# Two queues for the first reads, and another order of the first block's preparation, in a two-layer transformer kernel

## The chip, the cores and the metric

The kernel runs on one core of a Trainium2 chip. The metric is the device time of one launch in microseconds (us). The engines are TensorE (PE, with its weight loads PEld), VectorE (DVE), ScalarE (ACT), GpSimd (POOL) and SyncE (SP, which computes nothing and issues DMAs).

## The reference

Two layers, each an attention block and a gated block on 2048 tokens of 448 features, with the same weights in both layers:

```python
x = A_x                                     # [1, 2048, 448] f32
for _ in range(2):
    x = x + attention(layernorm(x))         # 16 heads of 28, qkv = x @ wqkv (448 x 1344), @ wo
    h = layernorm(x)
    x = x + (sigmoid(h @ w_gate) * (h @ w_up)) @ w_down      # inner size 1792
```

The layer norm has no scale and no offset. Everything is f32 in and out.

## The kernel before

**Number format.** Matrix products run on f16 operands. Each f32 operand is split into a high f16 part and a low f16 part (the f32 value less the high part), and a product is three matmuls: high by high, high by low, low by high. Weights are scaled by a power of two before the split; the power comes from the mean square of the matrix, so all of a weight block has to be read and squared before its first split. The features are four rows of 128: rows 0 to 2 are whole, row 3 holds 64 features, and its free half carries low parts (the "tail").

**Blocks.** The tokens are four blocks of four tiles of 128 tokens. For the projections a block has to stand with its features on the partitions, so its normalised tokens are turned.

**The order.** The kernel's order is written out by hand: each engine executes its instructions in program order, and DMAs issued by one engine enter one queue in that order. A read that reuses one of the completion semaphores waits in its issuing engine until the earlier transfer on that semaphore has landed. Buffers come from rings of slots (`big`, `qrt`).

**The head**, which the change touches, ends at the first projection matmuls:

- `load_x(t, n)` reads n token tiles from tile t on SyncE's queue. Tiles 0 to 3 (the first block) are read singly.
- `wq.read(j)` reads a third of wqkv (0 query, 1 key, 2 value) through `load_rows`; the query third in four pieces: two rows, one row, and the tail's 64 features twice.
- `first.stats(j)` takes mean and variance of a tile on DVE (`BATCH_NORM_STATS2`, `BATCH_NORM_AGGREGATE`) and the inverse root on POOL; `first.scale(t)` writes the normalised tile on DVE; `first.turn(t)` turns it on PE, four transposes into four PSUM banks, each bank holding one feature row of all four tiles.
- `first.turned_high(kts)` copies such banks as high parts (`xhl`); `first.turned_low(kts)` subtracts for the low parts, on DVE.
- `wq.measure_first(i)` squares and sums the query weights in three pieces (two on ScalarE, the last on DVE); `wq.sum_first(i)` adds them over the partitions on PE; `powers` makes the scale `up`.
- `wq.high_cols` scales weight columns to their high part on ScalarE, `wq.low_cols` makes the low part on DVE. `wq.measure(1)`, further on, squares the key weights on ScalarE.
- `keep_busy(n)` runs n matmuls of zeros (`still`) on PE, whose result nobody reads.

The first projection tile is eleven matmuls (`qkp`, line 564). Their order is that in which parts become ready: rows 0 to 2 of high by high, low parts of rows 0 and 1, the low weights, the low part of row 2, the tails.

Of the kernel before, what the change touches and what calls it, by code (L numbers as in the profile page):

```python
# [15 lines left out]
AF = mybir.ActivationFunctionType  # L16
# [3 lines left out]
P = 128  # L20
S = 2048
D = 448
# [5 lines left out]
TB = NT // NB  # L28
# [90 lines left out]
def interleaved_layers(ctx: ExitStack, tc: tile.TileContext, x_in, wqkv, wo, w_gate, w_up,  # L119
                       w_down, out):  # L120
    nc = tc.nc
# [6 lines left out]
    big = Slots(spool, "s", N_SLOTS)  # L128
# [22 lines left out]
    def bank(i, name):  # L151
        return psum(f"bank{i}", name, [P, 512])


    x = cpool.tile([P, NT, D], F32, name="x")
# [5 lines left out]
    warm = cpool.tile([P, 1], F32, name="warm")  # L161
# [10 lines left out]
    x_src = x_in[0].rearrange("(p t) d -> p t d", t=NT)  # L172
    x_dst = out[0].rearrange("(p t) d -> p t d", t=NT)

    def load_x(t, n):
        nc.sync.dma_start(x[:, t:t + n, :], x_src[:, t:t + n, :])

    nc.vector.memset(still, 0.0)
    nc.vector.memset(warm, 0.0)
    nc.scalar.activation(warm, warm, AF.Square)  # L180
    make_identity(nc, ident)
    nc.gpsimd.memset(nhalf, -0.5)
    nc.gpsimd.memset(ones, 1.0)
# [3 lines left out]
    def tables():  # L187


        nc.gpsimd.memset(ind_f, 1.0)  # L190
        for j in range(2):
            v = ind_f[:, 4 * j:4 * j + 4, :]
            off = -64 * j
            nc.gpsimd.affine_select(out=v, in_=v, compare_op=ALU.is_ge, fill=0.0, base=off,
                                    pattern=[[P, 4], [-DH, H]], channel_multiplier=1)
            nc.gpsimd.affine_select(out=v, in_=v, compare_op=ALU.is_ge, fill=0.0,
                                    base=DH - 1 - off, pattern=[[-P, 4], [DH, H]],
                                    channel_multiplier=-1)
        nc.gpsimd.memset(ind[:, 8:, :], 0.0)
        nc.gpsimd.tensor_copy(ind[:, 0:8, :], ind_f)  # L200
        qrt.put(ind_f)
        units = big.get("units", [2, S], F16)
        nc.gpsimd.memset(units, UNIT)
        nc.gpsimd.dma_start(unit_scr, units)
        big.put(units)


    def load_rows(dst, src, c0, n, queue=nc.sync, parted=False):

        for a, b in ((0, 2), (2, 3)) if parted else ((0, 3),):  # L210
            queue.dma_start(dst[:, a:b, :],
                            src[a * P:b * P, c0:c0 + n].rearrange("(s p) n -> p s n", p=P))
        queue.dma_start(dst[0:64, 3, :], src[384:448, c0:c0 + n])
        queue.dma_start(dst[64:128, 3, :], src[384:448, c0:c0 + n])

    def split(hi, lo, raw):

# [24 lines left out]
    def powers(c, n, squares):  # L242


        c = slice(c, c + n)
        nc.vector.tensor_scalar(pw[:, c], squares.bitcast(I32), 24, 23,
                                op0=ALU.logical_shift_right, op1=ALU.logical_shift_left)
        nc.vector.tensor_scalar(up.bitcast(I32)[:, c], pw[:, c], -1.0, float(203 << 23),
                                op0=ALU.mult, op1=ALU.add)
# [7 lines left out]
    def keep_busy(n=1):  # L257
        pm = bank(2, "still")
        for i in range(n):
            c = slice(P * (i % 4), P * (i % 4) + P)  # L260
            nc.tensor.matmul(pm, still[:, c], still, start=(i == 0), stop=(i == n - 1))

    class Block:
# [256 lines left out]
                nc.scalar.copy(self.raw[0:n, kt, :], pt[0:n])  # L520
            big.put(self.xn)

        def turned_high(self, kts=range(4), engine=None):
            for kt in kts:
                if kt not in self.pt:
                    continue
                to, pt = ((self.hi[:, kt, :], self.pt[kt]) if kt < 3 else
                          (self.tail[0:64], self.pt[kt][0:64]))
                if engine is nc.vector:
                    nc.vector.tensor_copy(to, pt)  # L530
                else:
                    nc.scalar.copy(to, pt)

        def turned_low(self, kts=range(4)):
            for kt in kts:
                if kt not in self.pt:
                    continue
                pt = self.pt[kt]
                if kt < 3:
                    nc.vector.tensor_tensor(self.lo[:, kt, :], pt, self.hi[:, kt, :],  # L540
                                            op=ALU.subtract)
                else:
                    nc.vector.tensor_tensor(self.tail[64:128], pt[0:64], self.tail[0:64],
                                            op=ALU.subtract)

        def drop(self):
# [53 lines left out]
    class WeightsQKV:  # L600
# [3 lines left out]

            self.raw = []

        def read(self, j):
            self.raw.append(big.get("wraw", [P, 4, D]))
            load_rows(self.raw[j], wqkv, j * D, D, parted=(j == 0))

        def measure_first(self, i):

# [10 lines left out]
        def sum_first(self, i):  # L623
            if i == 0:
                self.first = bank(3, "sums")[:, 0:1]
            nc.tensor.matmul(self.first, ones, first_sums[:, i:i + 1], start=(i == 0),
                             stop=(i == 2))
            if i == 2:
                powers(0, 1, self.first)

        def measure(self, j):
            junk = big.get("junk", [P, 4, D], BF16)
# [292 lines left out]
    class Measure:  # L925
# [9 lines left out]
        def read(self, n=1):  # L935
            for _ in range(n):
                kind, j = self.to_read.popleft()
                t = big.get("raw", [P, 2048])
                n = {"o": 4, "d": min(4, NF - 4 * j), "gu": 0}[kind]
                v = t[:, 0:n * D].rearrange("p (s n) -> p s n", n=D)  # L940
                queue = nc.sync if kind == "o" or j < 3 and kind == "d" else nc.gpsimd
                if kind == "gu":
                    v = t.rearrange("p (w s c) -> p w s c", w=2, s=4)
                    for i, w in enumerate((w_gate, w_up)):
                        load_rows(v[:, i], w, 0, 2 * P, queue)
                elif kind == "o":
                    load_rows(v, wo, 0, D, queue)
                else:
                    queue.dma_start(v, w_down[j * 512:j * 512 + n * P, :].rearrange(
                        "(s p) n -> p s n", p=P))  # L950
                self.rows.append((kind, t, n * D))
# [868 lines left out]
    expect_jump(0)  # L1820
    wq = WeightsQKV()
    wq.tiles()
    first = Block(0)
    begun = [first]
    for t in range(TB):
        load_x(t, 1)
    wq.read(0)
    wq.read(1)
    load_x(TB, TB)
    wq.read(2)  # L1830
    load_x(2 * TB, 2 * TB)
    keep_busy(11)
    wq.measure_first(0)
    first.begin()
    first.turn_banks(4, range(4))
    first.parts()
    first.stats(0)
    first.stats(1)
    for t in range(TB):
        first.scale(t)  # L1840
        first.turn(t)
        keep_busy(2)
        if t == 0:
            first.stats(2)
            first.stats(3)
    wq.sum_first(0)
    first.turned_high([0], nc.vector)
    wq.measure_first(1)
    wq.measure_first(2)
    wq.sum_first(1)  # L1850
    first.turned_high([1, 2])
    first.turned_low([0])
    keep_busy(2)
    wq.sum_first(2)
    tables()
    keep_busy(3)
    wq.high_cols(0, 0, P, slice(0, 1))
    wq.high_cols(0, 0, P, slice(1, 4))
    first.turned_high([3])
    wq.high_cols(0, P, D)  # L1860
    first.turned_low([1])
    wq.low_cols(0, 0, P)
# [3 lines left out]
    for layer in range(LAYERS):  # L1866
# [4 lines left out]
        wq = WeightsQKV()  # L1871
# [34 lines left out]
```

## Time and profile before

| | |
|---|---|
| median of three runs | 1894.76 us (1894.62 to 1895.75) |
| span of the profiled execution (its own time is not given) | 1893.0 us |
| PE busy | 1886.5 us of the span |
| DVE, ACT, POOL busy | 1430.7, 1382.7, 231.5 us |
| HBM read, written | 207.88 MB, 50.85 MB |
| granted TensorE clock | 1.000 |

The page gives busy time for the whole span. The head is read from the timeline, which lists instructions in order: start, duration, engine, line, operation, output and input, count, and in brackets how long the engine had been idle and what released it. Lines "SPq" are DMA issues, not transfers. The view by stretches gives each engine's busy time in a stretch, the granted clock, the share of the 16 DMA engines' time, and GB/s.

### The profile page before, as it was taken

What the parts mean: (1) busy time and instruction counts of PE and PEld (TensorE: products, weight loads), DVE (VectorE), ACT (ScalarE), POOL (GpSimd) and SP (SyncE); (2) the same over time, 40 slices, a digit from 0 to 9 for tenths busy, and PEclk for the clock granted to TensorE, in tenths of its full rate; (3) what the DMA queues carried; (4) which work ended last, traced back from release to release, by engine and by line L of the source; (5) the groups of instructions that cost most, each with busy time, mean ns of one, the idle gap of its engine ahead of it and who ended that gap; (6) DMA issues with size and microseconds to landing.
All of it is one profiled execution on the core that took longest, in us unless ns stands there. A gap on an engine that the chain in (4) does not pass through costs nothing. (4 is left out here: it accounts for less than half of the span.)

```text
span 1893.0 us, 56282 instructions
## 1 busy us (share of the span) xinstructions
PE 1886.5 (100%) x24254; PEld 1323.1 (70%) x24254; DVE 1430.7 (76%) x2835; ACT 1382.7 (73%) x1772; POOL 231.5 (12%) x453
## 2 busy tenths in 40 slices
PE   9999999999999999999999999999999999999999
PEld 4455555555556799999954556667666567999998
DVE  7758989898976688787564487787778676887664
ACT  5569999999993566555345799999999745565541
POOL 3023112222101111111100000000000020121110
PEclk9999999999999999999999999999999999999999
DMA  7676454334323566646734322122120245666553
GB/s 247 194 212 166 132 137 128 107 119 129 103 88 121 192 205 235 231 181 238 251 96 134 90 52 47 32 52 52 31 48 24 67 160 174 218 251 223 208 208 142
DMA packets 110882, 270.86 MB, mean 143 GB/s; under 512 B 13214, under 2 KB 67838, under 8 KB 110496
## 3 DMA queue, kind: packets, MB, share of 16 engines
q0 software_dynamic: 31776, 158.51, 23.4%
q1 hardware_dynamic: 78288, 108.20, 20.3%
q8 instruction: 192, 3.15, 0.7%
q10 hardware_dynamic: 560, 0.46, 0.1%
q14 instruction: 66, 0.54, 0.1%
HBM read 207.88 MB, written 50.85 MB: 137 GB/s over the span
## 5 line engine op out<-in xcount | busy, mean ns | idle before, releaser
L1222 ACT ACTIVATE prob_s<-sc 128x1536 f32<-128x1536 f32 (+1 forms) x657 | 887.9, 1487 | 6.6 <-PE sc L1207 5.9
L1258 PE MATMUL acc<-prob_s,val_s 128*32 128x256 f32 (+3 forms) x7700 | 569.9, 383 | 0.0
L1207 PE MATMUL sc<-qp_s 114*32 114x512 f16 x7868 | 553.2, 379 | 0.0
L579 PEld LDWEIGHTS <-gu_s 128*128 128x128 f16 x4368 | 426.9, 98 | 46.8 <-issue 0.4
L1207 PEld LDWEIGHTS <-qp_s 114*32 114x32 f16 x8192 | 272.7, 95 | 203.4 <-issue 88.3
L1258 PEld LDWEIGHTS acc<-prob_s,val_s 128*32 128x32 f32 x7700 | 272.3, 110 | 142.9 <-issue 13.6
L579 PE MATMUL chain<-xwide_s,gu_s 128*128 128x256 f16 x2016 | 247.5, 273 | 0.0
L1552 PE MATMUL dnp<-dn_s,hparts_s 128*128 128x224 f16 x2016 | 225.2, 259 | 0.0
L1552 PEld LDWEIGHTS <-hparts_s 128*128 128x128 f16 x2016 | 194.0, 98 | 4.4
L1238 DVE SCALAR_TENSOR_TENSOR power_q<-power_q,expo_q 128x512 f32<-128x512 f32 x243 | 168.2, 692 | 8.3
L1625 ACT COPY one_q<-chain 128x256 f32<-128x256 f32 x224 | 82.4, 371 | 121.4 <-PE chain L579 120.8
L1641 DVE TENSOR_TENSOR one_q<-side,one_q 128x512 f32<-128x512 f32 x112 | 72.2, 686 | 101.8 <-PE side L579 101.5
L579 PE MATMUL side<-xshort_s,gu_s 128*128 128x256 f16 x1120 | 140.5, 273 | 0.0
L564 PE MATMUL qkp<-xhl_s,wqk_s 128*128 128x512 f16 x616 | 138.1, 379 | 0.7 <-ACT wqk_s L231 0.2
L564 PEld LDWEIGHTS <-wqk_s 128*128 128x128 f16 x616 | 60.1, 98 | 69.8 <-ACT wqk_s L231 1.1
L1437 POOL DMA_DIRECT2D gu_s<-gu_parts x104 | 56.0, 538 | 430.5 <-PE side L579 424.5
L1287 DVE STREAM_TRANSPOSE oturned_q<-acc 128x512 f32<-128x512 f32 x32 | 22.9, 716 | 97.1 <-PE acc L1258 96.9
L1258 PE MATMUL acc<-power_q,val_s 128*32 128x256 f32 (+3 forms) x300 | 94.2, 396 | 0.0
L579 PE MATMUL side<-xwide_s,gu_s 128*128 128x256 f16 x672 | 91.6, 273 | 0.0
L1505 ACT CAST hparts_s<-hsums_q 128x256 f16<-128x256 f32 (+1 forms) x136 | 65.0, 494 | 30.2 <-DVE hsums_q L1517 20.2
L756 ACT ACTIVATE qkhl_q<-qkp 128x512 f16<-128x512 f32 x56 | 33.2, 593 | 71.9 <-PE qkp L564 68.3
L1652 ACT ACTIVATE one_q<-one_q 128x512 f32<-128x512 f32 x56 | 35.2, 629 | 64.3 <-DVE one_q L1641 64.3
(218 smaller groups left out, 2318.0 us busy)
## 6 DMA issues: line engine op xcount, KB each, us to landing
gu_s<-gu_parts POOLq DMA_DIRECT2D x104, 800.0 KB, 6.0
dn_s<-dn_parts POOLq DMA_DIRECT2D x42, 784.0 KB, 7.8
qp_s<-qk_scr SPq DMA_DIRECT2D x96, 224.0 KB
qk_scr<-qkhl_q SPq DMA_DIRECT2D x56, 256.0 KB
gu_parts<-pack_s POOLq DMA_DIRECT2D x14, 800.0 KB, 3.8
xt_scr<-xs_s SPq DMA_DIRECT2D x48, 224.0 KB
xraw_s<-xt_scr SPq DMA_DIRECT2D x12, 768.0 KB
qp_s<-qk_scr SPq DMA_DIRECT2D x64, 112.0 KB
```

Source lines behind the costliest of these rows:

```text
L564: nc.tensor.matmul(pm, w, x, start=(i == 0), stop=(i == len(terms) - 1))
L579: nc.tensor.matmul(pm, a, x, start=(first and i == 0), stop=(i == len(terms) - 1), skip_group_check=True)
L1207: nc.tensor.matmul(ps[32 * j:32 * j + 32, :], hd.k[:, keys], hd.q[:, qb * W:(qb + 1) * W], start=True, stop=True, tile_position=(0, 32 * j))
L1222: nc.scalar.activation(prob[:, 0:n, :], ps[:, 0:n, :], AF.Exp, scale=exp_scale)
L1238: nc.vector.scalar_tensor_tensor(p, p, c[k], y, op0=ALU.add, op1=ALU.mult)
L1258: nc.tensor.matmul(acc[qb * VC:(qb + 1) * VC, s], v[:, kc % TB, h, :], probs[c * NB + qb][:, s], start=(kc == 0 and a == 0), stop=(kc == N ...
L1437: queue.dma_start(self.gu[-1][m], gu_parts[p, m])
L1505: nc.scalar.copy(to[:, :, 0], a)
L1552: nc.tensor.matmul(pm, a[:, x, t], w[:, p, y], start=(begin and n == 0 and (j == 0 or alone)), stop=(n == 2), skip_group_check=True)
L1625: nc.scalar.copy(to, pm)
L1641: nc.vector.tensor_tensor(one[m], side[m], one[m], op=ALU.add)
L1652: nc.scalar.activation(out, v, AF.Sigmoid, scale=gate_scale)
```

## The change

The four single token tiles are now read by SyncE as the first thing in the program, and the query weights by ScalarE at the same time (`wq.read(0, nc.scalar)`); ScalarE's first activation, which loads its table, stands behind those reads. The key weights, tiles 4 to 7, the value weights and tiles 8 to 15 are read by SyncE behind `read_behind`: a one-column memset on DVE, placed after tile 2's statistics, into the slot that the key weights will take.

The squares of the query weights on ScalarE, and their sums on PE, now stand ahead of every copy of turned tiles on ScalarE; DVE's square of the last piece stands ahead of its first copy. The high copies are made in two halves: tiles 0 and 1 early, tiles 2 and 3 after the scale has been made; on ScalarE the second halves stand behind the first two weight scales. The statistics of tile 3 now follow the scale of tile 1. There are 17 zero matmuls in the head instead of 24. Behind the head every engine has the same instructions in the same order.

```diff
-    def load_x(t, n):
-        nc.sync.dma_start(x[:, t:t + n, :], x_src[:, t:t + n, :])
-
+    def load_x(t, n, queue=nc.sync):
+        queue.dma_start(x[:, t:t + n, :], x_src[:, t:t + n, :])
+
+    for t in range(TB):
+        load_x(t, 1)
     nc.vector.memset(still, 0.0)
     nc.vector.memset(warm, 0.0)
-    nc.scalar.activation(warm, warm, AF.Square)
...
-        def turned_high(self, kts=range(4), engine=None):
+        def turned_high(self, kts=range(4), engine=None, js=range(TB)):
+            c = slice(js[0] * P, (js[-1] + 1) * P)
...
+        def read_behind(self):
+
+            raw = big.get("wraw", [P, 4, D])
+            nc.vector.memset(raw[:, 0, 0:1], 0.0)
+            big.put_next(raw)
...
-            if i == 2:
-                powers(0, 1, self.first)
+
+        def scale_first(self):
+            powers(0, 1, self.first)
...
     wq.tiles()
+    wq.read(0, nc.scalar)
     first = Block(0)
     begun = [first]
-    for t in range(TB):
-        load_x(t, 1)
-    wq.read(0)
-    wq.read(1)
-    load_x(TB, TB)
-    wq.read(2)
-    load_x(2 * TB, 2 * TB)
-    keep_busy(11)
-    wq.measure_first(0)
+    nc.scalar.activation(warm, warm, AF.Square)
+    keep_busy(8)
     first.begin()
     first.turn_banks(4, range(4))
     first.parts()
     first.stats(0)
     first.stats(1)
     for t in range(TB):
+        if t == TB - 1:
+            wq.measure_first(2)
+            for i in range(3):
+                wq.sum_first(i)
+            first.turned_high([0], nc.vector, (0, 1))
+            keep_busy(1)
         first.scale(t)
         first.turn(t)
-        keep_busy(2)
         if t == 0:
             first.stats(2)
+            wq.read_behind()
+            wq.read(1)
+            load_x(TB, TB)
+            wq.read(2)
+            load_x(2 * TB, 2 * TB)
+            wq.measure_first(0)
+            wq.measure_first(1)
+        if t == 1:
+            first.turned_high(range(1, 4), None, (0, 1))
             first.stats(3)
-    wq.sum_first(0)
-    first.turned_high([0], nc.vector)
-    wq.measure_first(1)
-    wq.measure_first(2)
-    wq.sum_first(1)
-    first.turned_high([1, 2])
-    first.turned_low([0])
+        if t < TB - 1:
+            keep_busy(2)
+    wq.scale_first()
+    first.turned_high([0], nc.vector, (2, 3))
     keep_busy(2)
-    wq.sum_first(2)
     tables()
-    keep_busy(3)
     wq.high_cols(0, 0, P, slice(0, 1))
     wq.high_cols(0, 0, P, slice(1, 4))
-    first.turned_high([3])
+    first.turned_high([1, 2], None, (2, 3))
+    first.turned_low([0])
+    first.turned_high([3], None, (2, 3))
     wq.high_cols(0, P, D)
     first.turned_low([1])
     wq.low_cols(0, 0, P)
```

More of the change, by code (lines that the diff above doesn't have):

```diff
@@ L212, in load_rows @@
                             src[a * P:b * P, c0:c0 + n].rearrange("(s p) n -> p s n", p=P))
-        queue.dma_start(dst[0:64, 3, :], src[384:448, c0:c0 + n])
-        queue.dma_start(dst[64:128, 3, :], src[384:448, c0:c0 + n])
+        for r in (0, 64):
+            queue.dma_start(dst[r:r + 64, 3, :], src[384:448, c0:c0 + n])
     def split(hi, lo, raw):
@@ L526, in turned_high @@
                     continue
-                to, pt = ((self.hi[:, kt, :], self.pt[kt]) if kt < 3 else
-                          (self.tail[0:64], self.pt[kt][0:64]))
+                to, pt = ((self.hi[:, kt, c], self.pt[kt][:, c]) if kt < 3 else
+                          (self.tail[0:64, c], self.pt[kt][0:64, c]))
                 if engine is nc.vector:
@@ L532, in turned_high, with turned_low @@
                     nc.scalar.copy(to, pt)
-        def turned_low(self, kts=range(4)):
+        def turned_low(self, kts=range(4), js=range(TB)):
+            c = slice(js[0] * P, (js[-1] + 1) * P)
             for kt in kts:
@@ L537, in turned_low @@
                     continue
-                pt = self.pt[kt]
+                pt = self.pt[kt][:, c]
                 if kt < 3:
-                    nc.vector.tensor_tensor(self.lo[:, kt, :], pt, self.hi[:, kt, :],
+                    nc.vector.tensor_tensor(self.lo[:, kt, c], pt, self.hi[:, kt, c],
                                             op=ALU.subtract)
                 else:
-                    nc.vector.tensor_tensor(self.tail[64:128], pt[0:64], self.tail[0:64],
+                    nc.vector.tensor_tensor(self.tail[64:128, c], pt[0:64], self.tail[0:64, c],
                                             op=ALU.subtract)
@@ L605, in tiles, with read @@
             self.raw = []
-        def read(self, j):
+        def read(self, j, queue=nc.sync):
             self.raw.append(big.get("wraw", [P, 4, D]))
-            load_rows(self.raw[j], wqkv, j * D, D, parted=(j == 0))
+            load_rows(self.raw[j], wqkv, j * D, D, queue, parted=(j == 0))
+        def read_behind(self):
+            raw = big.get("wraw", [P, 4, D])
+            nc.vector.memset(raw[:, 0, 0:1], 0.0)
+            big.put_next(raw)
         def measure_first(self, i):
```

## The prediction

> **What bounds the kernel now.** I read the page first, then the busy time by stretches of the head, then the order of time there. The page: its span of 1893.0 us lies 1.76 us below the median of the three runs, 1894.76 us; the profiled execution's own time is not given, so I add a change of the span to the median.
>
> ```profile
> span 1893.0 us, 56282 instructions
> ...
> PE 1886.5 (100%) x24254; PEld 1323.1 (70%) x24254; DVE 1430.7 (76%) x2835; ACT 1382.7 (73%) x1772; POOL 231.5 (12%) x453
> ```
>
> TensorE has no rest of the span to hide anything in. The stretches (busy time and count by engine, granted clock, DMA share, GB/s):
>
> ```profile
> 0.00:5.00 5.00, 3.75 (x9) 1.34 (x10) 1.73 (x6) 1.49 (x2) 1.43 (x11) 1.00 0.55 159
> ...
> 2.50:3.50 1.00, 1.00 (x4) 0.44 (x3) 0.02 (x1) 0.00 (x0) 0.00 (x0) 1.00 1.08 375
> 3.50:5.00 1.50, 1.50 (x5) 0.46 (x4) 1.43 (x4) 0.00 (x0) 0.49 (x2) 1.00 0.79 215
> 5.00:10.00 5.00, 4.22 (x21) 2.47 (x20) 3.43 (x9) 0.93 (x2) 3.64 (x10) 1.00 1.02 301
> 10.00:15.00 5.00, 4.68 (x27) 2.48 (x26) 4.14 (x10) 4.09 (x10) 4.50 (x12) 1.00 1.05 324
> ...
> 25.00:30.00 5.00, 5.00 (x27) 2.58 (x26) 4.51 (x15) 3.51 (x7) 1.81 (x4) 1.00 0.31 105
> ```
>
> From 25 us PE is busy throughout, so a microsecond in the head is a microsecond at the end, and nothing behind the head is touched: its instructions stand in the same order on every engine. Up to 10 us the busy resource is the DMA, which outside the dip at 3.5 to 5 us is at a share of 1. What arrives, and what is issued, in order of time:
>
> ```profile
> 0.79 1.28 ACT L180 ACT_TABLE_LOAD   x1 [0.79 <-PEq L1893]
> 0.80 1.82 SPq L176 DMA_DIRECT2D x<-in_A_x_dram  x4
> ...
> 1.25 4.87 PE L261 MATMUL still<-still_q 128*128 128x512 f16 x11 [1.25 <-DVE warm L179]
> ...
> 2.65 0.94 SPq L211 DMA_DIRECT2D wraw_s<-in_A_wqkv_dram  x2
> ...
> 4.88 0.59 SPq L211 DMA_DIRECT2D wraw_s<-in_A_wqkv_dram  x1
> ...
> 5.92 1.08 PE L508 MATMUL turn<-ident,xn_s 128*128 128x128 f32 x4
> ...
> 6.79 0.74 PE L261 MATMUL still<-still_q 128*128 128x512 f16 x2
> ...
> 7.01 0.63 DVE L495 BATCH_NORM_STATS2 st<-x 128x6 f32<-128x448 f32 x1 [0.43 <-DMA x<-in_A_x_dram]
> ...
> 8.31 0.66 PE L508 MATMUL turn<-ident,xn_s 128*128 128x128 f32 x4 [0.78 <-DVE xn_s L320]
> ...
> 8.81 0.59 PE L261 MATMUL still<-still_q 128*128 128x512 f16 x2
> ...
> 9.07 0.95 ACT L620 ACTIVATE junk_q<-wraw_s 128x896 bf16<-128x896 f32 x1 [6.78 <-DMA wraw_s<-in_A_wqkv_dram]
> ...
> 10.93 0.58 SPq L176 DMA_DIRECT2D x<-in_A_x_dram  x1
> ```
>
> The fourth token tile is there at 7.01, the first half of the query weights at 9.07, and all of them just before 10.93 (that read waits in the program for the semaphore of their last piece). In bytes: a tile is 0.229 MB, the query weights 0.917 MB; so 0.917, 1.376 and 1.835 MB in order. The chain from there:
>
> ```profile
> 7.68 0.18 DVE L496 BATCH_NORM_AGGREGATE mv<-st 128x2 f32<-128x6 f32 x1
> ...
> 8.39 0.70 POOL L500 TENSOR_TENSOR rs<-rs,nhalf 128x1 f32<-128x1 f32 x1
> ...
> 9.12 0.51 DVE L320 TENSOR_SCALAR xn_s<-x,mv,rs 128x448 f32<-128x448 f32 x1 [0.44 <-POOL rs L500]
> ...
> 10.11 0.60 PE L508 MATMUL turn<-ident,xn_s 128*128 128x128 f32 x4
> ...
> 10.42 0.69 DVE L530 CAST xhl_s<-turn 128x512 f16<-128x512 f32 x1 [0.79 <-PE turn L508]
> ...
> 10.97 0.50 PE L626 MATMUL sums<-first_sums,ones 128*128 128x1 f32 x4
> ...
> 11.03 0.61 DVE L617 CUSTOM_DVE_ANT_0 junk_q<-wraw_s 128x448 bf16<-128x448 f32 x1
> ...
> 11.56 0.69 DVE L540 TENSOR_TENSOR xhl_s<-turn,xhl_s 128x512 f16<-128x512 f32 x1
> ...
> 12.35 0.15 DVE L248 TENSOR_SCALAR up<-pw 128x1 int32<-128x1 int32 x1
> ...
> 12.54 0.91 ACT L231 ACTIVATE wqk_s<-wraw_s,up 128x128 f16<-128x128 f32 x2 [0.91 <-DVE up L248]
> ...
> 12.99 2.41 PE L564 MATMUL qkp<-xhl_s,wqk_s 128*128 128x512 f16 x9 [0.20 <-ACT wqk_s L231]
> ...
> 13.48 0.75 DVE L234 SCALAR_TENSOR_TENSOR wqk_s<-wraw_s,up,wqk_s 128x512 f16<-128x512 f32 x1 [0.38 <-ACT wqk_s L231]
> ...
> 14.86 0.68 DVE L543 TENSOR_TENSOR xhl_s<-turn,xhl_s 64x512 f16<-64x512 f32 x1
> ...
> 15.08 1.69 ACT L633 ACTIVATE junk_s<-wraw_s 128x1792 bf16<-128x1792 f32 x1
> ...
> 15.60 2.97 PE L564 MATMUL qkp<-xhl_s,wqk_s 128*128 128x512 f16 x13 [0.20 <-DVE xhl_s L543]
> ```
>
> The first projection matmul is at 12.99, but the first tile can't end before DVE's last subtraction (L543) ends at 15.54: PE goes on at 15.60. That point is what I move. The tokens' own branch has room: cast at 10.42, before the weights' square at 11.03.
>
> **The change part by part.** *Transfers.* ScalarE issues its four weight reads from about 0.8 (its table load had that place; at 0.59 us for such an issue, four take 2.4, and the table load ends near 4.5, with ScalarE idle until 9.07 anyway: nothing). So weights start some 1.8 us sooner, but on DMA engines that x already fills. With equal turns the k-th part of x lands when twice its bytes have been moved: tile 1 (half of all) when 0.917 MB had arrived before, 7.0; tile 2 when 1.376 MB had, 9.1; tile 3 with the last weights. That end was 10.9. It comes forward by the dip: 21% of 1.5 us = 0.3. That gives 10.6, with 10.9 as the late bound. The early bound is the mean rate: 159 GB/s over 5 us are 0.8 MB, the rest at 301 GB/s is through at 8.45. [...] 8.45 + 1.6 less the dip is 9.7, which I take, since its row is the landing of the same tile; 8.45 and 10.9 stay for the range.
>
> [...]
>
> *From tile 3 (landing T) to PE's point.* DVE: statistics 0.85 (7.01 to 7.86). Then it has, in its new order, the scale of tile 2 (0.51), the square of the weights' last quarter (0.61), half a cast, and the scale of tile 3. A half cast has its nearest rows here:
>
> ```profile
> L1648 DVE TENSOR_TENSOR two_q<-side,two_q 128x256 f32<-128x256 f32 x112 | 42.2, 418 | 0.0
> L1625 ACT COPY two_q<-chain 128x256 f32<-128x256 f32 x112 | 41.2, 372 | 40.3 <-PE chain L579 39.9
> ```
>
> 0.42. So T + 2.4, past POOL's T + 2.1 (0.85 and 7.86 to 9.09). Scale to T + 2.9; 0.5 to the turned tile (9.63 to 10.42 less PE's queue), half cast 0.42: T + 3.8. Then five old steps in their old order: 0.69, 0.69, 0.75, 0.68, 0.68 = 3.5. PE's point is T + 7.4; break-even T is 8.2. At T = 9.7 it is 17.1: 1.5 later.
>
> *From the last weights (landing Tw).* The square now stands ahead of half cast, scale, turn, half cast and the five steps: 0.61 + 0.42 + 0.51 + 0.5 + 0.42 + 3.5 = Tw + 6.0, where before it was 10.9 + 4.7. With the weights at the same 9.7 that is 15.7: not last. The edit "weights squared ahead of all copies" therefore gains nothing while tile 3 is late; it puts a scale and two half casts behind Tw that lay ahead of it.
>
> *PE's queue, an added wait.* Turning tile 2 now writes banks of which ScalarE still copies the first half, so it waits for three half copies (3 x 0.37 = 1.1), and these stand on ScalarE behind both weight squares. Behind that wait on PE: two still matmuls, the three sums, one still matmul, turning tile 3. From tile 2 at 9.1: statistics 0.85, scale 0.51, turn 0.6, copies about 1.0, the rest of the turn and two stills 0.6, sums 0.5, still 0.2, turning to its first bank 0.3, half cast 0.42, 3.5: 17.6. With tile 2 0.5 sooner (dip and the rest of what moves T) 17.1. So this wait ends level with the DVE chain, and the two hide each other.
>
> *PE's pace.* The still matmuls ran at 4.87/11 = 0.44 us, those at 6.79 took 0.74 a pair, those at 8.81 0.59: PE speeds up after some 5.5 us of work, while the granted clock reads 1.00 all along. Eight instead of eleven end at 1.25 + 8 x 0.44 = 4.8, still at the slow pace, and the first turn now waits behind tile 1's statistics (DVE order): 7.0 + 0.85 + 0.51 = 8.4. PE rests 3.6 us. Slow, each group of turn and stills costs 1.08 + 0.44 instead of 0.6 + 0.44 and stands in the queue above: 0.5 for one, 1.3 for two and the last one. I take 0.7.
>
> *Reads held back.* SyncE's key-weight read now waits for a one-column memset behind tile 2's statistics, about 10; behind it in SP's queue stand six more reads and then the stores. Key weights, 0.917 MB at 324 GB/s = 2.8, land near 14.5; ScalarE's square of them comes at 15.08 + 2. The later tokens and values follow on a queue that stays full: covered by some 2 us; without that cover it would count in full. ScalarE has three half copies (1.1) between its first scales and that square, where one tail copy stood: 0.5 more in front of the first tile's evacuation, of which PE takes no notice as long as the next tile has another bank: nothing, or 0.5 if it had none. Removed stills (24 to 17) stood beside DVE's chain: nothing.
>
> Sum: 1.5 + 0.7 = 2.2 us: 1894.8 + 2.2 = 1897.0.
>
> **Rivals.** *The two queues move more together*, as the first row (375 GB/s) allows: by 2.5 us 0.1 MB had come (0.8 less 0.375 and 1.5 x 0.215), the other 1.73 MB take 4.6, with little lag T = 7.3. PE's point is then 14.7 by tile 3 and 13.3 by the weights: a gain of 0.9, 1893.9. For it: the dip, in which the single queue left engines idle. Against: 301 GB/s at a full share after it.
>
> *PE stays slow into the projection* (the other side). If rests keep interrupting it, the 13 matmuls that followed 15.60 take 13 x 0.44 = 5.7 instead of 2.97, 2.7 more, atop the forecast's 2.2 and, with T at 10.9, 1.2 again: 1899.7 to 1900.9. It decides if PE has not worked 5 us or so without a rest before 17 us. Against it: a slow PE takes longer over the turns and so rests less.
> [...]
>
> *It doesn't share*: SP's queue is served first, x lands as before, the weights at 10.6, their early issue idle. By the weights 16.6: plus 1.0, 1895.8.
>
> **How the numbers follow.** 0.2%, 3.8 us, is about what a measurement of this kernel can tell from no change. Forecast (1895.8 to 1898.5) 0.56; faster transfers 0.20, of which 0.02 goes past 3.8 us; slow PE 0.16, of which 0.14 lies beyond 3.8; no sharing 0.08. So faster 0.02, same 0.84, slower 0.14. The range holds the forecast with T from 8.5 to 10.9 and both ends of the pace, the third rival, and part of the first and the second: 1894.0 to 1899.2.
>
> **What would show it.** Right: tile 3's statistics start near 9.7 (7.01 before), a rest of PE of about 3 us before the first turn, the 13 matmuls near 17.8, and from there the same distances as before. Wrong: statistics before 8.2, a first turn before 6.5, or a projection that starts under 12.5; then the transfers, not the order on DVE, were mis-sized. If PE's point is late but the end isn't, something behind the head had room that I don't see.

## The result, and the profile after

| | before | after |
|---|---|---|
| median | 1894.91 us (1894.47 to 1895.75, 17 runs) | 1897.88 us (1895.93 to 1900.21, 17 runs) |
| ratio, 95% interval | | 1.0015 (1.0008 to 1.0022) |
| profiled execution: time, span | span 1893.0 us | 1895.96 us, span 1894.1 us |

The kernel is 2.97 us (0.16%) slower: the interval lies above 1, and the change inside the 0.2% that the prediction called no change. More telling than the median is the width: the runs of before lie within 1.3 us, those of after within 4.3. The profiled execution is one of the fastest, so its trace shows only the first 1.1 us of the loss. The page of after:

```profile
span 1894.1 us, 56273 instructions
...
PE 1885.7 (100%) x24247; PEld 1343.6 (71%) x24247; DVE 1431.3 (76%) x2837; ACT 1383.5 (73%) x1775; POOL 232.6 (12%) x453
```

After, by stretches (busy time and count of PE, PEld, DVE, ACT, POOL; granted clock, DMA share, GB/s):

```profile
2.50:3.50 1.00, 1.00 (x4) 0.44 (x3) 0.00 (x0) 0.40 (x1) 0.00 (x0) 1.00 0.83 269
3.50:5.00 1.50, 1.34 (x4) 0.16 (x2) 0.81 (x2) 1.09 (x2) 0.12 (x1) 1.00 1.05 404
5.00:10.00 5.00, 2.97 (x11) 1.92 (x12) 3.54 (x10) 2.05 (x6) 2.79 (x7) 1.00 0.68 180
...
8.00:9.00 1.00, 1.00 (x4) 0.15 (x3) 0.97 (x5) 0.00 (x0) 0.40 (x1) 1.00 0.01 2
```

The dip of before at 3.5 to 5 us (215 GB/s) is gone: 404. From 8 to 9 us nothing moves: tokens and query weights are there, and the next read, held back until DVE's memset at 8.40, is issued from 8.50. The order of time in after:

```profile
0.80 1.01 ACTq L212 DMA_DIRECT2D wraw_s<-in_A_wqkv_dram  x2
...
0.80 1.82 SPq L176 DMA_DIRECT2D x<-in_A_x_dram  x4
...
1.25 3.59 PE L262 MATMUL still<-still_q 128*128 128x512 f16 x8 [1.25 <-DVE warm L181]
...
5.73 0.63 DVE L496 BATCH_NORM_STATS2 st<-x 128x6 f32<-128x448 f32 x1 [0.95 <-DMA x<-in_A_x_dram]
...
7.03 1.11 PE L509 MATMUL turn<-ident,xn_s 128*128 128x128 f32 x4 [2.19 <-DVE xn_s L321]
...
7.60 0.63 DVE L496 BATCH_NORM_STATS2 st<-x 128x6 f32<-128x448 f32 x1 [0.63 <-DMA x<-in_A_x_dram]
...
7.94 1.06 PE L262 MATMUL still<-still_q 128*128 128x512 f16 x2
...
8.37 0.51 DVE L321 TENSOR_SCALAR xn_s<-x,mv,rs 128x448 f32<-128x448 f32 x1
...
8.80 0.62 DVE L496 BATCH_NORM_STATS2 st<-x 128x6 f32<-128x448 f32 x1
...
10.03 0.62 DVE L626 CUSTOM_DVE_ANT_0 junk_q<-wraw_s 128x448 bf16<-128x448 f32 x1
...
11.03 0.59 PE L262 MATMUL still<-still_q 128*128 128x512 f16 x2
...
15.79 0.68 DVE L546 TENSOR_TENSOR xhl_s<-turn,xhl_s 64x512 f16<-64x512 f32 x1
...
16.52 2.97 PE L567 MATMUL qkp<-xhl_s,wqk_s 128*128 128x512 f16 x13 [0.28 <-DVE xhl_s L546]
```

Tile 1's statistics wait for their tokens until 5.73 (4.25 before), tile 2's until 7.60. Tile 3's start at 8.80 (7.01), but not for want of tokens: all of them had landed by about 8.0, and DVE first had tile 2's statistics and, at 8.37, the scale of tile 1. PE ends its zero matmuls at 4.84, rests 2.19 us, and is then at half pace (1.06 a pair of zero matmuls, 0.59 from 11.03) until about 10.6. Its second stretch of projection matmuls starts at 16.52, 0.92 later than before, and the span is 1.1 longer. I call that start PE's point.

### The profile page after: what moved, and what is told of

Same layout as the page of the kernel before. It is cut to its first block, busy times and chain, and to the rows that moved or that the text cites. A ratio compares the mean times of both kernels' runs of the same rounds, so it can differ in the third digit from the quotient of the medians.

```text
span 1894.1 us, 56273 instructions
## 1 busy us (share of the span) xinstructions
PE 1885.7 (100%) x24247; PEld 1343.6 (71%) x24247; DVE 1431.3 (76%) x2837; ACT 1383.5 (73%) x1775; POOL 232.6 (12%) x453
## 5 line engine op out<-in xcount | busy, mean ns | idle before, releaser
L1217 PEld LDWEIGHTS <-qp_s 114*32 114x32 f16 x8192 | 283.9, 96 | 192.8 <-issue 77.7
L1268 PEld LDWEIGHTS acc<-prob_s,val_s 128*32 128x32 f32 x7700 | 283.5, 110 | 133.3 <-issue 12.5
```

The source lines that it names most:

```text
L1217: nc.tensor.matmul(ps[32 * j:32 * j + 32, :], hd.k[:, keys], hd.q[:, qb * W:(qb + 1) * W], start=True, stop=True, tile_position=(0, 32 * j))
L1268: nc.tensor.matmul(acc[qb * VC:(qb + 1) * VC, s], v[:, kc % TB, h, :], probs[c * NB + qb][:, s], start=(kc == 0 and a == 0), stop=(kc == N ...
```

## The experiments

Theory A: the rest before the first turn costs PE its pace, for a time that differs between executions. Theory B: the two queues land at varying times. Times are medians; "before" is the kernel before in the same comparison. With eleven executions of a version, the 95% interval reaches some 0.09% (1.7 us) to either side: e2, e3, e4, e6, e8 and e10 are slower beyond it, while e1, e5, e7, e9 and e11 can't be told from before.

### PE's rest filled (e1_filled)

```diff
-    keep_busy(8)
+    keep_busy(14)
```

> The changed kernel with 14 instead of 8 zero matmuls at the start, so that PE works until about 7.4 us, when the first turn is due. Theory A (PE's rest before the first turn leaves it slow for longer, by a different amount in each run): the median comes down from about 3.0 us above the kernel before to 0.3 to 1.2 above, and the runs lie within some 1.5 us of one another instead of 4.3. Theory B (the two queues land at varying times, and that spreads the runs): median and spread stay, about 3 us above and 4 us wide.

1895.57 us (1894.95 to 1896.01) against 1895.30: 0.3 slower, runs within 1.1 us. PE in this kernel:

```profile
1.25 6.15 PE L262 MATMUL still<-still_q 128*128 128x512 f16 x14 [1.25 <-DVE warm L181]
7.20 0.65 PE L509 MATMUL turn<-ident,xn_s 128*128 128x128 f32 x4
...
16.25 2.97 PE L567 MATMUL qkp<-xhl_s,wqk_s 128*128 128x512 f16 x13 [0.28 <-DVE xhl_s L546]
```

Six matmuls that compute nothing take away most of the loss and most of the spread, while tile 3's statistics start as late as in after (8.90). Theory B falls. Before is not free of long executions either: in this comparison 5 of its 33 took 1897.6 to 1899.5 us.

### The rest alone, in the kernel before (e4_few_stills)

```diff
-    keep_busy(11)
+    keep_busy(4)
```

> The kernel before with 4 instead of 11 zero matmuls at the start, nothing else: they end near 3.0 us and PE rests about 2.9 us until the first turn at 5.9. Theory A: 0.5 to 3 us slower, runs spread over 3 to 4 us, and the zero matmuls behind the turns still at 0.43 us apiece beyond 9 us. Theory B: no difference above 0.2 us, spread 1.3 us, since the zero matmuls compute nothing.

1897.92 us (1896.07 to 1899.98) against 1895.30: 2.6 slower, 3.9 us wide. The lost pace by itself costs nearly what the whole change costs. In its trace PE's point is 2.0 later and the span 2.8 longer, so 0.9 is lost behind the head, which these experiments leave open. Its PE:

```profile
1.25 1.89 PE L261 MATMUL still<-still_q 128*128 128x512 f16 x4 [1.25 <-DVE warm L179]
5.88 1.11 PE L508 MATMUL turn<-ident,xn_s 128*128 128x128 f32 x4 [2.74 <-DVE xn_s L320]
...
9.61 1.06 PE L261 MATMUL still<-still_q 128*128 128x512 f16 x2
...
17.56 2.96 PE L564 MATMUL qkp<-xhl_s,wqk_s 128*128 128x512 f16 x13 [0.20 <-DVE xhl_s L543]
```

### One queue, else as changed (e2_one_queue)

```diff
-    wq.read(0, nc.scalar)
+    wq.read(0)
```

> The changed kernel with the query weights read by SyncE again, behind the four token tiles; order, half copies, held-back reads and 8 zero matmuls as changed. If shared transfers are what delays the tokens: tile 3's statistics start near 7.0 instead of 8.8, the first turn near 6.0 instead of 7.0 (a rest of PE of about 1 us), the weights are complete near 10, and PE's second stretch of projection matmuls starts near 16.3, about 0.7 us above the kernel before. Theory A adds little for such a short rest (0 to 1 us, runs 1 to 3 us wide); theory B expects the spread of the kernel before, 1.3 us. If sharing is not it, the first turn stays near 7.0.

1898.19 us (1896.88 to 1899.48) against 1895.30: 2.9 slower. The first turn went to 5.88 as expected (7.03 in after), so sharing had delayed it; the time did not follow. This execution took exactly the median, and its clock shows why:

```profile
4.00:7.40 3.40, 1.79 (x8) 0.58 (x6) 2.63 (x9) 0.00 (x0) 1.80 (x5) 1.00 0.96 316
7.40:10.80 3.40, 2.55 (x10) 1.34 (x11) 2.51 (x8) 2.39 (x7) 2.93 (x8) 0.57 0.93 262
10.80:14.20 3.40, 3.40 (x16) 2.68 (x16) 0.90 (x4) 0.68 (x2) 3.02 (x6) 0.50 1.05 317
14.20:17.60 3.40, 3.40 (x9) 1.21 (x8) 3.29 (x8) 3.40 (x6) 2.22 (x9) 0.50 1.16 360
17.60:21.00 3.40, 3.40 (x16) 1.55 (x15) 2.46 (x4) 1.78 (x4) 0.00 (x0) 0.93 0.99 399
```

The granted clock is half for some 10 us, into the projection: the first two tiles ran as one slow stretch.

```profile
15.05 6.42 PE L567 MATMUL qkp<-xhl_s,wqk_s 128*128 128x512 f16 x22
```

### The second queue alone (e3_queue_alone, e6_queue_filled)

In the kernel before, the query weights on ScalarE:

```diff
-    nc.scalar.activation(warm, warm, AF.Square)
...
-    wq.read(0)
+    wq.read(0, nc.scalar)
+    nc.scalar.activation(warm, warm, AF.Square)
```

> The kernel before with one part of the change: the query weights read by ScalarE from the start, its table load behind them; all else as before, 11 zero matmuls too. By the landings of the changed kernel (tile 3 at 8.6 us) and the chain of before from there, PE's second stretch starts near 16.4 instead of 15.6: 0.6 to 1.0 us slower. Theory A: zero matmuls end at 6.1 and the first turn is at 7.0, so PE stays at pace and the runs lie within 1.5 us. Theory B: runs spread over about 4 us, median 2 to 3 us slower.

1898.58 us (1896.77 to 1900.21) against 1895.30: 3.3 slower, 3.4 wide. The width looked like theory B. But PE rested twice (1.86 and 1.95 us), began fast and fell back:

```profile
6.96 0.66 PE L507 MATMUL turn<-ident,xn_s 128*128 128x128 f32 x4 [1.86 <-DVE xn_s L319]
...
9.99 0.66 PE L507 MATMUL turn<-ident,xn_s 128*128 128x128 f32 x4 [1.95 <-DVE xn_s L319]
...
12.79 1.06 PE L507 MATMUL turn<-ident,xn_s 128*128 128x128 f32 x4
```

I had counted the first rest only. So the same with both filled:

```diff
-    keep_busy(11)
+    keep_busy(14)
...
-        keep_busy(2)
+        keep_busy(7 if t == 0 else 2)
```

> The kernel before with only the query weights on ScalarE (as in the run with that one part), and zero matmuls added so that PE does not rest: 14 at the start, 7 behind the first turn. Theory A: the 3.3 us of that run fall to what the later tokens cost, 0.6 to 1.0 us, PE's second stretch near 16.4, and the runs lie within 1.5 us. If the two queues themselves cost the 3.3 us, they stay.

1897.60 us (1896.90 to 1898.19) against 1895.04: the width is gone (1.3), but 2.6 remain, where I expected 0.6 to 1.0.

```profile
10.00 0.66 PE L507 MATMUL turn<-ident,xn_s 128*128 128x128 f32 x4 [0.96 <-DVE xn_s L319]
...
17.29 2.97 PE L563 MATMUL qkp<-xhl_s,wqk_s 128*128 128x512 f16 x13 [0.20 <-DVE xhl_s L542]
```

In the order of before, the statistics of tiles 2 and 3 stand ahead of tile 1's scale on DVE; with shared transfers the second turn waits for both tiles (10.00 against 8.31), and the rest follows: PE's point 1.7 later. The span is 2.3 longer; the 0.6 between came behind the head and stay unexplained. The change's own order lets tile 1 go first.

### The order alone, PE filled (e8_order_filled)

One queue, as e2, with 12 zero matmuls at the start and 4 behind each of the first three turns.

```diff
-    wq.read(0, nc.scalar)
+    wq.read(0)
...
-    keep_busy(8)
+    keep_busy(12)
...
-            keep_busy(2)
+            keep_busy(4)
```

> The changed kernel with the query weights on SyncE behind the tokens and PE filled (12 zero matmuls at the start, 4 behind the first three turns): the new order and the held-back reads without the second queue and without PE's rest. By the step that counts from the last weights (9.5 us in the unfilled run, plus 6.0) PE's second stretch starts near 15.5, so the time is that of the kernel before within 0.4 us, and below the filled two-queue version by 0.3 to 0.7. If the second queue costs nothing, the two filled versions agree.

1897.51 us (1895.52 to 1899.71) against 1895.04: 2.5 slower, and 4.2 wide in spite of the filling. This misses the expectation. The profiled execution (1896.43 us) has PE's point at 17.23, and two delays on DVE, the second beside a memset on POOL:

```profile
10.26 0.62 DVE L626 CUSTOM_DVE_ANT_0 junk_q<-wraw_s 128x448 bf16<-128x448 f32 x1 [1.94 <-DMA wraw_s<-in_A_wqkv_dram]
...
10.99 1.79 POOL L204 MEMSET units_s<- 2x2048 f16 x1
...
11.15 1.89 DVE L321 TENSOR_SCALAR xn_s<-x,mv,rs 128x448 f32<-128x448 f32 x1
```

The square of the last weights waits for them until 10.26, and tile 3's scale stands behind it. That scale then took 1.89 us instead of 0.51: it began 0.16 us after a memset on POOL and ended 0.26 after it. PE waited 1.36 us in the middle of turning tile 2 for ScalarE's copies. Its other executions were not traced, but the three longest (1898.24 to 1899.71) report a mean granted clock of 0.998: 0.002 of 1893 us lost at half clock are, as an estimate, some 7.6 us, so there PE lost its pace again. So each old part with one new one took about 2.5 us here, e8 with some pace lost, and both new parts together, with PE filled, 0.3: it seems that the two parts need each other, and for the change as a whole the pace is the loss left over.

### Reads not held back, PE filled (e7_not_held)

```diff
-    keep_busy(8)
+    keep_busy(14)
...
-            wq.read_behind()
```

> The changed kernel with PE filled (14 zero matmuls) and the later reads not held back: no memset, so that the key weights follow the tokens on SyncE's queue. If holding back matters: tokens and query weights complete 0.3 to 1 us later than with it (8.7 us), and the time is 0.3 to 1 us above that of the filled version. If it does not: within 0.2 us of it.

1895.39 us (1894.76 to 1896.22) against 1895.04: 0.35 slower, as e1's 0.3. With PE filled, holding back neither gains nor costs anything measurable. PE's point:

```profile
16.42 2.97 PE L567 MATMUL qkp<-xhl_s,wqk_s 128*128 128x512 f16 x13 [0.28 <-DVE xhl_s L546]
```

### Between (e9_eleven)

```diff
-    keep_busy(8)
+    keep_busy(11)
```

> The changed kernel with 11 zero matmuls at the start, between its own 8 (PE rests 2.2 us before the first turn, median 3.0 us slower) and the 14 that leave no rest (0.3 slower): they end near 6.0, a rest of 1.0. If what counts is the length of the rest, the median lies between, 0.5 to 2 us slower, with runs between 1.5 and 4 us apart. If any rest there does it: 2.5 to 3 us. If 11 are enough as in the kernel before: 0.2 to 0.5.

1896.61 us (1895.43 to 1897.88) against 1895.10: 1.5 slower, 2.5 wide, between 8 and 14 zero matmuls in both. In its profile PE had got up to pace (11 zero matmuls in 4.08 us), rested 2.09 us, and fell back to half, with a granted clock of 0.56 in the stretch from 7.4 us:

```profile
7.40:10.80 3.40, 2.89 (x11) 1.65 (x12) 2.51 (x8) 0.66 (x4) 1.96 (x5) 0.56 0.27 34
10.80:14.20 3.40, 3.39 (x22) 2.29 (x20) 2.54 (x8) 1.30 (x5) 3.13 (x9) 0.94 1.00 330
```

### The changed kernel again (e10_after_again, e12_after_third)

> The changed kernel unaltered, on the chip of these runs, for a second profile of it: the first was one of its fastest executions (1895.96 us). Theory A: median 2.5 to 3.2 us slower, 4 us apart, and where the profiled execution is near the median, the zero matmuls and turns behind 10 us, or the projection matmuls, are still at 0.43 us apiece. If its loss lies behind the head, PE's second stretch starts near 16.5 as before and the time still is 2 us longer.

1898.31 us (1896.29 to 1900.66) against 1895.10: 3.2 slower. The profile is again of the fastest execution (1896.29). Its clock was at half for one such stretch:

```profile
7.40:10.80 3.40, 3.39 (x12) 2.02 (x13) 2.69 (x8) 0.80 (x5) 2.07 (x6) 0.50 0.26 37
10.80:14.20 3.40, 3.09 (x22) 2.24 (x21) 2.68 (x9) 1.41 (x5) 3.19 (x9) 1.00 1.05 339
```

> The changed kernel unaltered, one more look: the two profiles so far are of fast executions (1895.96 and 1896.29 us), in which PE is at full pace from about 10.6 us. Theory A: if this execution is near the median (1898), PE is slow over a stretch of about 3.4 us more, so that the turns of tiles 2 and 3 or the first projection matmuls run at 0.43 us apiece, and PE's second stretch starts 1.5 to 2.5 us later than 16.5. If it is again below 1896.5, it looks like the first two. If it is slow with PE's second stretch at 16.5, theory A fails.

One execution each: 1896.52 us against 1894.88. PE's point is at 16.45, like the first two's, but that is only 0.85 of the 1.6 us by which the span is longer; the other 0.75 came behind the head and stay unexplained. So not all of a loss arises in the head. And no execution of the changed kernel near its median was traced. What stands in for one is e2's, and the mean granted clock, which every execution reports: 0.997 in the slowest of both sets (1900.21 and 1900.66), as in e2's trace. 0.003 of 1893 us lost at half clock are, as an estimate, some 11 us, three stretches of 3.4. Many other long executions report 0.999 or 1.0, though: a PE that hasn't come up to pace since the start need not show in that number (it reads 1.00 for after's first 10 us, in which the pairs took 1.06).

### Versions meant to beat both (e5_tokens_first, e11_before_filled)

Tokens first on both queues, weights split over both, reads held, order of before, PE filled:

```diff
-        load_x(t, 1)
-    wq.read(0)
...
-    keep_busy(11)
+        load_x(t, 1, (nc.sync, nc.scalar)[t % 2])
+    wq.read_first()
+    nc.scalar.activation(warm, warm, AF.Square)
+    keep_busy(12)
...
-        keep_busy(2)
+        keep_busy(5 if t == 0 else 1)
...
-    first.turned_high([0], nc.vector)
     wq.measure_first(1)
     wq.measure_first(2)
+    first.turned_high([0], nc.vector)
```

> A version meant to beat both: the order of the kernel before with whole copies, but the four token tiles spread over SyncE and ScalarE ahead of the query weights (two pieces on each), the later reads held behind tile 2's statistics, the square of the last weights ahead of the first copy, and zero matmuls placed so that PE does not rest before the second turn (12, then 5, 1, 1). If transfers and order set the head: tile 3's statistics start before 7, the weights are complete near 8.8 (as in the changed kernel), PE's second stretch of projection matmuls starts at 13.5 to 14.0 instead of 15.6, and the time is 1.5 to 2 us below the kernel before, near 1893. If PE's pace sets it, and it is lost again, 1 to 3 us above.

1895.21 us (1894.79 to 1896.22) against 1895.04: the same.

```profile
4.25 0.63 DVE L494 BATCH_NORM_STATS2 st<-x 128x6 f32<-128x448 f32 x1 [3.05 <-DMA x<-in_A_x_dram]
...
9.37 0.51 DVE L319 TENSOR_SCALAR xn_s<-x,mv,rs 128x448 f32<-128x448 f32 x1 [0.44 <-POOL rs L499]
...
15.20 2.96 PE L563 MATMUL qkp<-xhl_s,wqk_s 128*128 128x512 f16 x13 [0.20 <-DVE xhl_s L542]
```

PE's point is 0.4 earlier, not 1.6 to 2.1: once transfers no longer end last, statistics on DVE and POOL do, as they already did for tile 3 in after (tile 3's scale at 9.37, 9.12 before), and with two tiles at once the first came later (4.25, 3.48 in before).

```diff
-        keep_busy(2)
+        keep_busy(4 if t == 0 else 2)
```

> The kernel before with two more zero matmuls behind the first turn, where PE rests 0.8 us. Single executions of the kernel before took 1897.4 to 1899.5 us (6 of 66). Theory A: they too are executions in which PE lost its pace over that rest; filled, the median stays within 0.2 us and no execution is over 1896.5. If the rest has nothing to do with it, one in ten still is.

1895.69 us (1894.81 to 1896.01) against 1895.10. None of 11 executions was over 1896.5, but only 1 of 27 of before was in this comparison: inconclusive; the median is 0.6 higher, a miss. No version beat the kernel before measurably.

## Why the prediction was right or wrong

Predicted 1897.0 us, 1894.0 to 1899.2, no change at 0.84; measured 1897.88. The mechanisms were the right ones, late tokens and a PE out of pace, but both terms of the sum were mis-sized: 1.5 for the tokens and the order is 0.3 (e1), 0.7 for the pace is 2.7. That the total still came within 0.9 us was luck.

- **Transfers: far too pessimistic.** Tile 3 was put at 9.7. Everything had landed by about 8.0, before even the early bound of 8.45. The step that failed is the landing's lag of 1.6 behind a mean rate taken from 5 to 10 us. The 1.6 is 7.0, where tile 3 was there in before, less 5.4, where its 0.917 MB are through at 159 and then 301 GB/s; no run shows that a last landing trails by as much with two queues, with which the stretch from 3.5 to 5 us ran at 404 GB/s. This is the faster-transfers rival in part (375 assumed, T = 7.3). Tile 1 and tile 2 did come later beside the weights: their statistics started at 5.73 and 7.60 (4.25 and 5.74 in before). The 404 against 215 GB/s from 3.5 to 5 us can be issue time in part: in before, SyncE issued pieces of 0.115 MB some 0.6 us apart at 3.64 and 4.25, about 190 GB/s. No run separates that part from the rest.
- **T + 7.4: right from the start of the statistics, not from the landing.** From 8.80 it is 7.7 in after and, at pace, 7.4 in e1 (statistics at 8.90, 16.25). (The terms shown add up to 7.3.) But the sum let the statistics start at T. With T at 8.0 it would have given 15.4, a gain; DVE was behind by 0.8, with tile 2's statistics and tile 1's scale in front. Landing and DVE's queue together were worth 1.5 in the sum and are worth 0.65 at PE's point and 0.3 in the time of e1.
- **Weights not last, held-back reads covered: right.** e7 shows the second. That each old order with the new queue (e6) or new order with the old queue (e8) would cost about 2.5 was not foreseen; Tw + 6.0 left out a scale beside POOL's memset (7.0 in e8).
- **PE's pace: 0.7 was mis-sized.** after less e1, each against its own before, is 2.97 - 0.27 = 2.7. The mechanism and the rest were foreseen (3.6 us predicted, 2.19 measured in after, 2.93 in e10). The price was one fixed value for slow turns, with the same 0.44 for a group's two zero matmuls at either pace; in after such a pair took 1.06 slow and 0.59 at pace, so a group cost nearly twice the 0.5 put down. And the length of the slow time varies, up to 10 us in e2's execution.
- **The slow-PE rival** asked whether PE comes back before the projection. In e2 it did not. Two of after's 17 executions lie within its price of 1899.7 to 1900.9, one of them with a mean clock of 0.997; whether PE was slow into the projection there was not traced.
- **How long PE stays slow, and after what rest.** The clocks of the stretches put the half clock at 3.4 us in e3, e9 and e10 and at 10.2 in e2 (estimates: what the stretches lack of a clock of 1.00, taken as lost at e10's 0.50). It came with rests of 2.09 us in e9, 2.93 in e10, 1.86 and 1.95 in e3, and 1.18 and 0.6 in e2.

## What to carry to other kernels

A change that brings work later can cost more through the engine's pace than through the work (here 2.7 us against 0.3): look at where PE rests before its first useful matmuls, fill that rest, and judge the rest of the change only then. Where the runs of a kernel are suddenly wide, the profiled execution may be one that was spared; look at the distribution and the paces before explaining the median from its trace. Parts of a reordering that cost alone can pay for each other (2.6 and 2.5 us alone, 0.3 together), so undoing one part does not price it.

## What the runs showed of the hardware

- What a rest of PE costs differs between executions: the same program took 1895.93 to 1900.21 us; with the rest filled 1894.95 to 1896.01. That chance decides how long PE stays slow is argued from these times; no execution of the changed kernel near its median was traced.
- PE lost its pace with rests of 2.09 us (e9) and of 1.18 and 0.6 (e2), and its busy time in a stretch of 3.4 does not tell when. It kept its pace with 2.0 us of work (e8, 7.4 to 10.8 us; the next four zero matmuls took 1.03) and lost it with 1.8 (e2, 4.0 to 7.4); but e3, with 1.5 in each, kept it through 7.4 to 10.8 (granted clock 0.99) and lost it only in the next stretch (0.51).
- A DVE scale that began just after a memset on POOL over 2 partitions (1.79 us) took 1.89 us instead of 0.51 and ended 0.26 after the memset (one execution of e8). What held it the trace doesn't show.
